# Gated linear attention, then a hard-swish MLP, on one core: the decayed keys of every chunk transposed on TensorE, under a new order of all engines

## The chip, the cores and the metric

The kernel runs on one core of a Trainium2 chip. The time is the device time of one execution in microseconds (us). Before the change the median of 7 runs is 567.04 us (565.08 to 570.57).

## The reference

The first half is a recurrence over 768 tokens for 4 batches of 8 heads with 48 dimensions; the second half is an MLP on the 3072 tokens that come out.

```python
state = zeros((B, H, D, D))                       # B 4, H 8, S 768, D 48
for t in range(S):
    state = alpha[:, :, t, :, None] * state + einsum('bhd,bhe->bhde', k[:, :, t], v[:, :, t])
    y[:, :, t] = einsum('bhd,bhde->bhe', q[:, :, t], state)
x = y.transpose(0, 2, 1, 3).reshape(3072, 384)
h = x @ w_in                                      # 384 -> 2048
g = h * clip(h + 3.0, 0.0, 6.0) / 6.0
out = g @ w_out                                   # 2048 -> 384
```

## The kernel before

**Tiling.** The tokens are cut into 24 chunks of 128 (six for each batch, numbered j from 0). Two chunks make a group g of 256 tokens, so there are 12 groups. A chunk goes through the recurrence in its parallel form: a scan over alpha gives the decay R, keys are multiplied by R and queries by its counterpart P, scores are masked, and a state of 48x48 per head is handed to the next chunk of the batch. A group then goes through the MLP. Groups 0 and 1 use plain matrix products while the weights (float64 in DRAM, taken as pairs of 32-bit words) are still being loaded and converted; from group 2 on both products run as Strassen-like schemes with fewer multiplications, so that DVE makes sums of the weights, of x and of the products.

**Steps.** Everything is written as short steps, and one long string of words, read from left to right, fixes the order of the instructions on every engine. No scheduler moves anything afterwards: an engine executes its own instructions in the order of the words and waits in place where data or a buffer isn't there. The words that matter here are:

- `la.j`, `lk.j`, `lq.j`, `lv.j.z`: loads of a chunk's alpha, keys, queries and values, all on SP's DMA queue (L256 for the first six chunks, L267 for the others, L276 and L277 for the values); `w.i`: a sixteenth of the weights, on the same queue (L174, L177), converted by `d1`, `d2`, `dx` on ACT, `d3` on DVE and `d4` on POOL.
- `ta`, `tk`, `tq`: for chunks 0 to 5 a transpose on TensorE into PSUM (L288); from chunk 6 on a DVE transpose in 32x32 blocks, since the load already put the blocks in place (L292).
- `r.j`, `p.j`: the scans on DVE (L315, L326); `k.j`, `q.j`: the products with the decays on DVE (L338); `sc.j`: scores on TensorE (L346); `m.j`: masks on DVE (L352); `yi.j`, `yx.j`: the chunk's output on TensorE (L440, L450); `cy.j`: its copy out of PSUM on ACT (L458, L459).
- `u.j`: the update of the state on TensorE (L410), which needs the decayed keys with tokens on the partitions, that is a 128x128 transpose of each of the four head pairs; `sm.j` adds it to the state on DVE (L423, L425), `st.j` decays it on POOL (L397). The last chunk of each batch (5, 11, 17, 23) has no update.
- `M`, `n`, `o`, `e`, `h`: the first product of a group and its gate (TensorE L592, ACT L598, DVE L529 to L533, ACT L487, DVE L491); `P`, `K`, `G`, `s`, `O`: the second product (TensorE L692, ACT L671, DVE L708 and ACT L705, DVE L639 and L656, store L713). `f`, `fa`, `fb`, `fr`, `fg`, `b`: the products of groups 0 and 1 (TensorE L471, L482, L509). `z.m.n`: n products of the identity with itself on TensorE (L524), whose result nobody reads; they stand in the first 40 us.

**The transposed keys before the change.** For chunks 0 to 4 the words `kb.j` and `ck.j` make them: four TensorE transposes into a PSUM bank of the pool `t` (four banks, shared with `ta`, `tk`, `tq`, the two banks of scores, `u` and the two banks of `y`) and an ACT copy of 128x512 to SBUF.

```python
def k_by_token(j):                                  # kb
    if not last(j):
        t = bank("kb", j)
        for p in range(NP):
            nc.tensor.transpose(t[:, p], K_t[j][:, p], ident)
def keep_k(j):                                      # ck
    if not last(j):
        kb_t[j] = wk.tile([C, NP, C], FP, tag="kb", name="kb")
        nc.scalar.copy(out=kb_t[j], in_=ps_t.pop(("kb", j)))
```

For chunks 6 and up that have an update (15 of them) the words `kt.j`, `kw.j` and `kr.j` take their place: a DVE transpose in 32x32 blocks into the chunk's own load buffer (L380), four DMAs of 64 KB to a DRAM tile called `far` (L387) and one DMA of 256 KB back (L391). All five DMAs are issued on SP's queue, in line with the loads.

## Time and profile before

| | before |
|---|---|
| median of 7 runs | 567.04 us |
| the profiled execution, its own time | 565.55 us |
| the profiled execution, its span | 563.7 us |
| ACT busy | 196.7 us (35%) |
| POOL busy | 55.8 us (10%) |
| DMA queue of SP and its share of the 16 engines | 48.19 MB, 40.2% |
| granted TensorE clock over the span | 0.999 |

The span runs from the first to the last instruction of the profiled execution; 1.85 us of its time lie outside of it. PE is TensorE's matrix products, PEld its loads of weights, which overlap them; DVE, ACT and POOL are the vector, scalar and general engines; SP only issues DMAs here. The end of a matmul is modelled and one overlaps the next, so the distance from one start to the next says more of its price than its duration. A wait is named by who waited, for whom, the microseconds in total, the number of times and the longest.

### The profile page before, as it was taken

The numbers are of one execution on the slowest core, as the hardware profiler recorded it, in microseconds if no ns is written. First come the engines' busy times: TensorE is split into PE (matmuls) and PEld (weight loads), VectorE is DVE, ScalarE is ACT, GpSimd is POOL, SyncE is SP. The second block draws the span as 40 slices with busy tenths as digits, with TensorE's granted clock in tenths as the row PEclk, the third lists the DMA queues.
The fourth block names the chain that finished last, engine by engine and source line by source line (L and its number), as shares of the span: only waits on it lengthen the run. The fifth ranks groups of instructions, "written<-read, shape, count | busy, mean of one in ns | idle before, by whom it ended". The sixth has DMA issues, their size and how long they took to land.

```text
span 563.7 us, 12762 instructions
## 1 busy us (share of the span) xinstructions
PE 550.8 (98%) x5236; PEld 510.5 (91%) x5236; DVE 470.2 (83%) x798; ACT 196.7 (35%) x348; POOL 55.8 (10%) x70
## 2 busy tenths in 40 slices
PE   8899999999899998999999999999999999999997
PEld 7687977699799988999999999999999999999997
DVE  7886997999999998998998978976999977754580
ACT  1476665002322333322423422432421432432420
POOL 2333445100001000100000000000000000000000
PEclk9999999999999999999999999999999999999999
DMA  9999777104524636164264353162163340000000
GB/s 148 188 174 205 203 208 197 32 16 89 132 74 96 141 74 148 52 141 88 63 150 104 76 123 82 20 165 59 45 144 81 83 121 8 1 22 8 1 30 21
DMA packets 121270, 53.73 MB, mean 95 GB/s; under 512 B 80636, under 2 KB 114172, under 8 KB 121212
## 3 DMA queue, kind: packets, MB, share of 16 engines
q1 hardware_dynamic: 114588, 48.19, 40.2%
q10 hardware_dynamic: 6624, 4.72, 2.5%
q8 instruction: 41, 0.67, 0.5%
q14 instruction: 17, 0.14, 0.1%
HBM read 44.24 MB, written 8.65 MB: 94 GB/s over the span
## 4 chain that ended last, share of the span: by engine, by line
PE 86%; DMA 10%; DVE 2%; SPq 1%; issue 1%; ACT 0%; DVEq 0%; ACTq 0%
PE m_ps L692 35%; PE m_ps L592 28%; PE m_ps L471 5%; DMA rings<-in_k_dram 4%; PE m_ps L509 4%; PE y_ps L440 3%; PE sc_ps L346 3%; PE y_ps L450 2%; DMA t<-in_v_dram 2%; PE m_ps L482 2%; PE u_ps L410 2%; DMA kb<-far 1%; DMA aq<-in_alpha_dram 1%; PE tk_ps L288 1%; DMA far<-kq 1%
## 5 line engine op out<-in xcount | busy, mean ns | idle before, releaser
L692 PE MATMUL m_ps<-w,g_sb 128*128 128x192 f32 x704 | 121.2, 328 | 0.0
L692 PEld LDWEIGHTS m_ps<-w,g_sb 128*128 128x128 f32 x704 | 113.8, 190 | 2.3 <-issue 1.4
L598 ACT COPY g_sb<-m_ps 128x512 f32<-128x512 f32 x110 | 64.3, 584 | 139.0 <-PE m_ps L592 120.6
L692 PE MATMUL m_ps<-rings,g_sb 128*128 128x192 f32 x528 | 91.2, 326 | 0.0
L692 PEld LDWEIGHTS m_ps<-rings,g_sb 128*128 128x128 f32 x528 | 85.7, 190 | 0.0
L592 PE MATMUL m_ps<-xc,w 128*128 128x128 f32 x640 | 83.1, 278 | 0.2 <-ACT g_sb L598 0.2
L592 PEld LDWEIGHTS m_ps<-xc,w 128*128 128x128 f32 x640 | 77.2, 192 | 3.3 <-issue 1.6
L487 ACT ACTIVATE r<-g_sb,half 128x512 f32<-128x512 f32 x80 | 55.5, 719 | 55.3 <-DVE g_sb L529 22.5
L491 DVE SCALAR_TENSOR_TENSOR g_sb<-r,g_sb 128x512 f32<-128x512 f32 x80 | 54.4, 698 | 7.5 <-PE m_ps L692 4.3
L397 POOL TENSOR_TENSOR t<-t,R 128x384 f32<-128x384 f32 x20 | 20.9, 1045 | 382.9 <-DVE t L425 205.6
L592 PE MATMUL m_ps<-xT,raw 128*128 128x128 f32 x400 | 51.8, 276 | 0.0
L592 PEld LDWEIGHTS m_ps<-xT,raw 128*128 128x128 f32 x400 | 48.7, 192 | 0.3
L529 DVE TENSOR_TENSOR g_sb<-m_ps,g_sb 128x512 f32<-128x512 f32 x30 | 20.4, 684 | 27.9 <-ACT g_sb L598 27.2
L592 PE MATMUL m_ps<-xT,w 128*128 128x128 f32 x320 | 41.9, 278 | 0.0
L639 DVE TENSOR_TENSOR g_sb<-g_sb 128x512 f32<-128x512 f32 (+1 forms) x55 | 41.7, 793 | 0.1
L592 PEld LDWEIGHTS m_ps<-xT,w 128*128 128x128 f32 x320 | 38.2, 192 | 1.2 <-issue 0.2
L352 DVE TENSOR_TENSOR A<-sc_ps,mask 128x512 f32<-128x512 f32 x48 | 30.8, 683 | 2.5 <-PE sc_ps L346 2.1
L592 PE MATMUL m_ps<-xc,raw 128*128 128x128 f32 x240 | 32.1, 277 | 0.7 <-ACT g_sb L598 0.7
L471 PE MATMUL m_ps<-xT,w 128*128 128x256 f32 x144 | 32.8, 382 | 0.0
L315 DVE TENSOR_TENSOR_SCAN R<-t,ones 128x516 f32<-128x516 f32 x24 | 29.4, 1224 | 3.1 <-ACT t L306 2.8
L529 DVE TENSOR_TENSOR g_sb<-g_sb 128x512 f32<-128x512 f32 x40 | 27.0, 679 | 5.5 <-ACT g_sb L598 5.4
L592 PEld LDWEIGHTS m_ps<-xc,raw 128*128 128x128 f32 x240 | 29.9, 192 | 1.2 <-ACT g_sb L598 0.9
(110 smaller groups left out, 704.4 us busy)
## 6 DMA issues: line engine op xcount, KB each, us to landing
raw<-in_moe_w_out_dram SPq DMA_DIRECT2D x8, 768.0 KB
t<-in_v_dram SPq DMA_DIRECT2D x48, 96.0 KB
raw<-in_moe_w_in_dram SPq DMA_DIRECT2D x24, 192.0 KB
out_dram<-oh ACTq DMA_DIRECT2D x44, 96.0 KB
far<-kq SPq DMA_DIRECT2D x60, 64.0 KB
kb<-far SPq DMA_DIRECT2D x15, 256.0 KB
kq<-in_k_dram SPq DMA_DIRECT2D x36, 96.0 KB
aq<-in_alpha_dram SPq DMA_DIRECT2D x36, 96.0 KB
```

Source lines behind the costliest of these rows:

```text
L315: nc.vector.tensor_tensor_scan(out=reverse(R, n - 1, n), data0=reverse(ax, n, n), data1=reverse(ones, n, n), initial=0.0, op0=ALU.mult, op ...
L352: nc.vector.tensor_tensor(out=A_t[j][:, NP * o : NP * (o + 1)], in0=ps_t.pop(("sc%d" % o, j)), in1=mask.unsqueeze(1).to_broadcast([C, NP, ...
L397: nc.gpsimd.tensor_tensor(out=st[j % 2], in0=sm[j % 2], in1=R_t[j][:, :, 0:1].to_broadcast([C, NP, 2 * D]), op=ALU.mult)
L471: nc.tensor.matmul(h[:, f], w1[:, kk, o : o + C], xT_t[g][:, kk], start=(kk == 0), stop=(kk == KT - 1))
L487: nc.scalar.activation(out=to, in_=h, func=AF.Relu, bias=half, scale=1.0 / 6.0)
L491: nc.vector.scalar_tensor_tensor(out=to, in0=r, scalar=1.0, in1=h, op0=ALU.min, op1=ALU.mult)
L509: nc.tensor.matmul(o_t[c], gs[0][:, f, c * C : (c + 1) * C], w2[:, f], start=(f == 0), stop=(f == NF - 1))
L529: eng.tensor_tensor(out=out, in0=in0, in1=in1, op=ALU.add if s1 > 0 else ALU.subtract)
L592: nc.tensor.matmul(acc[g][i][:, f * C : (f + 1) * C], spots[w][:, f * C : (f + 1) * C], x_of(g, x), start=(first and f == 0), stop=last, s ...
L598: nc.scalar.copy(out=slots[z], in_=acc[g][i])
L639: nc.vector.tensor_tensor(out=out, in0=in0, in1=in1, op=ALU.subtract)
L692: nc.tensor.matmul(to[g], a, rhs[:, f], start=(first and f == 0), stop=(last and f == HF - 1), skip_group_check=True)
```

## The change

The words `kt`, `kw` and `kr`, their functions and the pool in DRAM go. The words `kb` and `ck` now also stand for the 15 chunks that used them, so all 20 chunks with an update get four TensorE transposes and an ACT copy. The whole string of words is replaced by another one; besides the words named, the words and their numbers are the same, apart from the choice of PSUM banks and SBUF slots (the last number of several words) and the `z` words, whose products go from 28 to 33. The order differs everywhere: in the loads at the start, in which sixteenth of the weights comes first, in how far ahead chunks are prepared (chunk 13's keys, queries and scores come within group 4's products instead of group 5's), in the place of each product.

```diff
-    far = ctx.enter_context(tc.tile_pool(name="far", bufs=2, space=bass.MemoryType.DRAM))
...
-    def turn_k(j):
-        to = k_in_blocks(j).rearrange("r (v p c) -> r p v c", v=V, p=NP)
-        nc.vector.transpose(out=to, in_=K_t[j].rearrange("r p (v s) -> r p v s", v=V))
...
-    def write_k(j):
...
-    def read_k(j):
...
-        "kt": turn_k, "kw": write_k, "kr": read_k, "u": update, "sm": next_state, "yi": within, "yx": across, "cy": keep_x,
+        "u": update, "sm": next_state, "yi": within, "yx": across, "cy": keep_x,
...
-        run("""la.0 z.3.5 lq.0 lk.0 lk.1 ta.0 la.1 ca.0 tq.0 r.0 lv.0.0 tk.0 lq.2 p.0 tk.1 z.0.2
-            la.2 k.0 ta.1 q.0 z.0.1 lq.1 ca.1 sc.0 r.1 la.3 tq.2 z.0.5 m.0 lv.3.1 k.1 w.1 ta.2
...
-            xc.2.7 G.1.3 kt.6 O.1.3 xc.2.8 kw.6 tq.6 xc.2.9 y.14 M.2.7.1 n.2.0.8 xc.2.2 y.22
-            M.2.1 p.6 n.2.7.9 M.2.8 lv.6.1 n.2.1.10 o.2.4.0 M.2.2 q.6 e.2.4 y.24 sc.6 n.2.2.11
-            xc.2.10 G.1.2 ca.7 kr.6 O.1.2 M.2.3 m.6 lk.7 M.2.18.2 M.2.4 r.7 n.2.18.12 M.2.17
-            n.2.4.13 lq.7 h.2.4 M.2.19 o.2.0.0 p.7 u.6 e.2.0 M.2.9 lq.8 h.2.0 M.2.5 tk.7 yi.6
...
+        run("""la.0 z.3.5 lk.1 lq.0 la.1 ta.0 la.2 ca.0 tk.1 r.0 lk.2 tq.0 lk.0 p.0 ta.1 z.0.2 ca.1
+            lv.1.0 q.0 ta.2 r.1 z.0.2 ca.2 lq.1 tk.2 z.0.2 k.1 lv.0.1 tk.0 p.1 z.0.6 lv.3.2 k.0
+            sc.0 la.3 tq.1 w.3 r.2 z.0.7 q.1 m.0 kb.0 z.0.2 ck.0 k.2 sc.1 lq.2 p.2 ta.3 la.4 m.1
...
+            kb.6 h.2.4 la.9 M.2.2 ck.6 y.22 M.2.17 tq.7 n.2.2.11 u.6 y.24 lk.9 M.2.3 r.7
...
+            s.6.5 P.6.0.3 xc.7.7 m.16 ca.19 u.15 K.6.0 M.7.2 G.6.0 sm.15 O.6.0 P.6.2 n.7.2.15
+            st.16 r.18 M.7.3 K.6.1 p.18 P.6.4 M.7.4 M.7.7.0 n.7.4.14 kb.16 n.7.7.12 M.7.5 tk.18
+            ck.16 M.7.8 n.7.5.13 k.18 lk.20 u.16 o.7.0.0 sc.17 sm.16 e.7.0 M.7.9 st.17 lv.19.2
+            m.17 M.7.18.1 lq.19 h.7.0 yi.17 o.7.1.0 n.7.18.14 r.19 e.7.1 M.7.10 lv.18.0 yx.17
...
```

## The prediction

> **What bounds the kernel now.** I read the page's first part, then the stages, the waits, and last the prices of single steps. The first table has one row for each stretch: its length, then busy time and count for each engine, then the granted clock, the DMA share and GB/s.

> ```profile
> span 563.7 us, 12762 instructions
> ...
> 0.00:60.00 60.00, 54.05 (x580) 46.53 (x581) 45.41 (x75) 30.84 (x41) 20.03 (x31) 1.00 1.10 176
> 60.00:120.00 60.00, 60.00 (x417) 46.43 (x417) 54.22 (x77) 25.53 (x38) 20.19 (x24) 1.00 0.50 146
> 120.00:240.00 120.00, 116.11 (x1166) 109.92 (x1165) 115.73 (x200) 38.17 (x72) 6.35 (x5) 1.00 0.41 95
> 240.00:540.00 300.00, 300.00 (x2951) 287.24 (x2950) 245.74 (x435) 99.41 (x191) 9.19 (x10) 1.00 0.32 75
> ```

> The columns after the length are PE, PEld, DVE, ACT, POOL. From 240 us on PE has no hole at all, while DVE is at 82% and ACT at 33%. Between 120 and 240 us PE misses 3.89 us and DVE is nearly as full (96%). In the first 60 us PE misses 5.95 us, with the DMA engines full. So PE's own work sets the end, and the only time that a new order can win is in the first 240 us. The chain of waits says the same: 86% of it is PE.

> Next is who waits for the trip that goes, and for the loads behind it.

> ```profile
> PE u_ps L410 <- DMA aq<-in_alpha_dram: 1.6, 1, 1.6
> PE m_ps L524 <- POOL ident masks.py:199: 1.5, 1, 1.5
> ...
> PE u_ps L410 <- DMA kb<-far: 0.9, 1, 0.9
> ```

> PE waited twice at `u` for a DMA. The second is the read from `far` by name (chunk 6, near 143 us). The first is chunk 8's, near 219 us. `u` doesn't read alpha; its `kb<-far` was issued at 215.79 and the alpha loads just after it, so I read the name as a mistaken landing and count this wait to the same trip. All 13 other reads landed under cover.

> **The prices.** Groups by line first (busy us, mean ns of one | idle before), then PE's timeline around two of the existing `kb` steps (start, duration), then a product block from the chain.

> ```profile
> L380 DVE STREAM_TRANSPOSE kq<-k 128x512 f32<-128x512 f32 x15 | 10.6, 704 | 0.1
> L363 PE MATMUL kb_ps<-ident,k 128*128 128x128 f32 x20 | 3.1, 278 | 0.0
> L368 ACT COPY kb<-kb_ps 128x512 f32<-128x512 f32 x5 | 2.9, 588 | 7.1 <-PE kb_ps L363 7.1
> ```

> ```profile
> 30.36 0.60 PE L363 MATMUL kb_ps<-ident,k 128*128 128x128 f32 x4
> 30.69 1.42 PEld L482 LDWEIGHTS m_ps<-xT,w 128*128 128x128 f32 x12
> 30.80 1.50 PE L482 MATMUL m_ps<-xT,w 128*128 128x128 f32 x12
> ```

> ```profile
> 86.03 0.60 PE L363 MATMUL kb_ps<-ident,k 128*128 128x128 f32 x4
> 86.56 1.08 PE L440 MATMUL y_ps<-A,t 128*32 128x128 f32 x32
> 87.57 0.56 PE L410 MATMUL u_ps<-t,kb 128*48 128x48 f32 x16
> ```

> ```profile
> 114.33 0.89 PE m_ps L592 x8
> ```

> Four transposes are four instructions, one each, and the next block starts 0.44 us (30.36 to 30.80) or 0.53 us (86.03 to 86.56) after the first of them. A product `M` is written as four matmuls and runs as eight instructions in 0.89 us, so 0.111 us each; a `z` product (56 instructions for 28) is 0.222 us.

> **Added: 15 `kb` on PE.** 15 x 0.49 us (the middle of 0.44 and 0.53) = **+7.35 us**, ends 6.6 and 8.0. By the stages above nothing hides them from 240 us on. In the old order chunks 6 to 9 are scored before about 200 us, so at most four of the 15 (2.0 us) can fall into holes of the 120 to 240 us stretch; I count none as hidden.

> The group row gives 278 ns for one transpose, start to end. [...]

> **Added: 15 `ck` on ACT.** 15 x 0.588 = 8.8 us, off the path: ACT is busy 33% where PE is full. What it delays are the copies `n` queued behind it, and through their PSUM banks the next `M`; that is in the term for new waits.

> **Removed: 15 `kt` on DVE.** 10.6 us of busy time. From 240 us on DVE isn't the limit, worth 0. Before that it is near it, and four of them are 2.8 us; but the new order also draws chunk 13's transposes, scans and products (about 7 us of DVE work: 3 x 1.1, 1.4, 1.2, 2 x 0.7) from group 5 into group 4, and more sums of weights ahead of `P.1.4`, so DVE is relieved less in the crowded part than the removal says. I take 0; ends -2.8 and 0.

> **Removed: the trip.** SP loses 60 writes and 15 reads, each about 0.6 us of issue, and the waits of the writes for DVE, behind which loads stood:

> ```profile
> SPq L387 <- DVE kq L380: 44.1, 6, 14.4
> ...
> DVE k L292 <- DMA kq<-in_k_dram: 4.8, 4, 1.8
> ```

> SP waited long, but the loads behind it cost DVE only 4.8 us in four waits and PE nothing directly. PE gets back the two waits at `u`: 1.6 + 0.9 = 2.5, **-2.5 us**; ends -2.5 and 0 (0 if another wait takes the place).

> [...]

> **Moved: the start.** Up to the end of the first weight sixteenth SP loads 11 pieces of 0.197 MB and 0.786 MB before (2.95 MB), 12 and 0.786 after (3.15 MB): 0.2 MB, 1.1 us at 176 GB/s. Up to the sixth sixteenth it is 8.66 MB against 8.85. PE's words without `z` ahead of the product of that sixteenth are about 42 us in both. I take 0. Ends: -4.5 (the 5.95 us missing in the first 60, less the 1.47 before the first matmul) and +4.5 (one sixteenth later, 0.786 MB at 176 GB/s). The five more `z` are 1.1 us that fill waiting; 0, ends 0 and +1.1. The last group's words are the same, 0.

> **New waits.** `kb` waits for a bank, `ck` for `kb`, `u` for `ck`, where before `u` had only to find the read landed. At 86.03 to 87.57 this chain was paid in 1.54 us, with only 1.01 us of `yi` between. In the new order the shortest covers are two products, 1.78 us (chunks 6, 16, 18), at 16 with an `n` ahead of `ck` (+0.58). Chunk 17's `yi` has 1.78 us of products behind its scores, while DVE has `sm.16` and `m.17` to do (0.7 + 1.37). Behind a `yi` or `u` that waits stand all later products on PE. I take **+1.5 us**, three such places at 0.5; ends 0 and 9 (0.6 us, an ACT instruction that is in the way, for each of 15 chunks).

> **Sum.** 7.35 - 2.5 + 1.5 = +6.35. Against the profiled execution's own 565.55 us this is 571.9. That execution lies 1.49 us under the median of 567.04, so the median goes to 573.4.

> **Rivals.**

> *A wait for the new chain decides.* The row for it is ACT's 7.1 us of waiting for `kb` in front of five copies; against it, PE waited only some 0.2 to 0.4 us for ACT there, and all but a few places have over 2 us of cover. With 9 instead of 1.5: 573.4 + 7.5 = 580.9. It decides from 0.4 us a chunk.

> *The waiting that goes pays for most.* The trips, the rest of the 3.89 us and half of the start's 4.5: 567.04 + 7.35 - 3.89 - 2.25 = 568.3, no measurable difference. For it: DVE at 96% there loses four `kt`. Against it: the work drawn forward.

> *The new order of the start makes it faster.* One mechanism: loads and weights come so that PE never waits in the first 60 us and half of the 28 `z` (6.2 us) give way to work. 567.04 + 7.35 - 3.89 - 4.5 - 3.1 = 562.9. It decides only if over 10.2 us (7.35 and the 2.84 of half a per cent) are won of the 14.6 that exist there at all. Against it: the `z` grow to 33, and the loads ahead of the first weights grow.

> *The change doesn't do what it says*, that is, the transposes are hidden: the 300.00 of 300 us excludes it for 11 of 15. Only four hidden: 573.4 - 2.0 = 571.4, inside the forecast.

> **How the numbers follow.** The forecast (570 to 577) 0.60; the chain of new waits (577 to 586) 0.17; most is paid back 0.14; faster 0.09. About 0.5%, 2.8 us, is what a measurement of this kernel can tell from no change, so faster means under 564.2 and slower over 569.9: 0.09, 0.14, 0.77. The predicted time is the likeliest case's, 573.4. The range 566.5 to 580 leaves out the faster case and the upper part of the new waits.

> **What would show it.** Right: 80 instructions at L363, PE's blocks of four transposes 0.44 to 0.53 us apart from the next start, PE full from 240 us on, no wait at L410 for a DMA, SP's queue smaller by the 75 DMAs, ACT 8 to 9 us busier, DVE some 10 us less. Wrong: holes in PE after 240 us at `yi`, `u` or `kb` (then the second case), or PE's first product of the MLP several us earlier than 28.9 us and a full PE between 120 and 240 us (then the faster cases).

## The result and the profile after

The changed kernel takes 569.26 us (median of 26 runs, 568.15 to 569.80), the kernel before 567.02 us (68 runs, 563.96 to 572.26). The ratio is 1.0034, with a 95% interval of 1.0019 to 1.0049: 1.1 to 2.8 us slower, the likeliest 1.9. The forecast was 573.4 us and 6.35 us slower. The direction was right and the size three times too large. Not foreseen at all: the changed kernel's runs lie within 1.7 us of each other, those of the kernel before within 8.3.

The profiled execution took 568.15 us and its span is 566.3. First the stages of the kernel after, in the columns of before (length; busy time and count of PE, PEld, DVE, ACT, POOL; granted clock, DMA share, GB/s).

```profile
0.00:60.00 60.00, 54.58 (x593) 46.46 (x594) 49.80 (x80) 32.70 (x45) 20.09 (x33) 1.00 1.14 186
60.00:120.00 60.00, 60.00 (x427) 47.59 (x426) 55.96 (x84) 23.61 (x36) 17.23 (x23) 1.00 0.56 157
120.00:240.00 120.00, 119.33 (x1238) 112.37 (x1237) 117.30 (x192) 40.45 (x78) 4.59 (x5) 1.00 0.32 78
240.00:540.00 300.00, 299.87 (x2906) 287.18 (x2905) 234.29 (x412) 103.95 (x197) 10.52 (x10) 1.00 0.20 51
```

PE missed 3.89 us between 120 and 240 us before; now it misses 0.67. From 240 us on it is as full as before (0.13 us missing), so the new steps brought no wait there. The first 60 us look much alike (5.42 against 5.95 us).

The groups of the added steps, then all of PE's own waits except those under 0.3 us:

```profile
L362 PE MATMUL kb_ps<-ident,k 128*128 128x128 f32 x80 | 12.1, 273 | 0.0
L367 ACT COPY kb<-kb_ps 128x512 f32<-128x512 f32 x20 | 11.9, 593 | 13.1 <-PE kb_ps L362 13.0
```

```profile
PE tq_ps L287 <- DMA rings<-in_q_dram: 2.2, 2, 1.7
PE m_ps L499 <- POOL ident masks.py:199: 1.5, 1, 1.5
PE tk_ps L287 <- DMA rings<-in_k_dram: 0.8, 2, 0.5
PE ta_ps L287 <- DMA rings<-in_alpha_dram: 0.5, 1, 0.5
PE m_ps L567 <- DVE g_sb L504: 0.4, 1, 0.4
```

There are 80 transposes instead of 20, none with idle time before it, and no update waits for a DMA. Counting from the start of each block to the start of the next, the transposes take 9.7 us of PE in this trace and 2.4 in that of before: +7.3. The same count over all blocks, against the price that such a block has when PE is full (near the shortest that occurs), gives the time that PE loses: 26.6 us before, 21.8 after, of which 11.8 and 9.3 lie in the first 60 us and 8.3 and 4.9 between 120 and 240 us. These are counts over all starts of the trace, not a row of it; the totals depend on the price that is taken, the difference of 4.8 little (4.3 to 5.6 us with prices from the shortest to the median). The fillers `z` are 10 instructions more, at 0.11 us each 1.1 us. Of the 7.3, 6.5 are the transposes' price when PE is full (60 at 0.109 us from start to start) and 0.8 the switches between blocks, which the count of lost time contains: 6.5 + 1.1 - 4.8 = 2.8, against the 2.6 between the two spans. So the transposes cost what was forecast, and about 5 us came back instead of the net 1.0 of the forecast.

### The profile page after: what moved, and what is told of

It is laid out like the page before. It is cut to its first block, busy times and chain, and to the rows that moved or that the text cites. A ratio compares the mean times of both kernels' runs of the same rounds, so it can differ in the third digit from the quotient of the medians.

```text
span 566.3 us, 12769 instructions
## 1 busy us (share of the span) xinstructions
PE 557.2 (98%) x5306; PEld 516.8 (91%) x5306; DVE 468.3 (83%) x783; ACT 204.7 (36%) x363; POOL 52.4 (9%) x70
## 4 chain that ended last, share of the span: by engine, by line
PE 93%; DMA 3%; DVE 2%; SPq 1%; ACT 0%; issue 0%; DVEq 0%; ACTq 0%
PE m_ps L667 35%; PE m_ps L567 31%; PE m_ps L446 6%; PE sc_ps L345 4%; PE y_ps L415 4%; PE m_ps L484 4%; PE y_ps L425 2%; PE m_ps L457 2%; PE u_ps L385 1%; DMA rings<-in_k_dram 1%; PE kb_ps L362 1%; PE m_ps L499 1%; DMA rings<-in_alpha_dram 1%; SPq L266 1%; PE tk_ps L287 0%; DMA aq<-in_alpha_dram 0%
## 5 line engine op out<-in xcount | busy, mean ns | idle before, releaser
L567 PE MATMUL m_ps<-xc,w 128*128 128x128 f32 x640 | 84.3, 279 | 0.4 <-DVE g_sb L504 0.4
L462 ACT ACTIVATE r<-g_sb,half 128x512 f32<-128x512 f32 x80 | 57.5, 723 | 72.1 <-DVE g_sb L508 37.4
L504 DVE TENSOR_TENSOR g_sb<-g_sb 128x512 f32<-128x512 f32 x40 | 28.2, 716 | 4.3 <-ACT g_sb L573 4.2
L325 DVE TENSOR_TENSOR_SCAN P<-t 128x516 f32<-128x516 f32 x24 | 30.6, 1273 | 0.1
```

Of the source, the lines that this page charges most:

```text
L325: nc.vector.tensor_tensor_scan(out=P_t[j], data0=aX[j % 2][:, 0:n], data1=ini[j % 2], initial=0.0, op0=ALU.mult, op1=ALU.add)
L462: nc.scalar.activation(out=to, in_=h, func=AF.Relu, bias=half, scale=1.0 / 6.0)
L504: eng.tensor_tensor(out=out, in0=in0, in1=in1, op=ALU.add if s1 > 0 else ALU.subtract)
L567: nc.tensor.matmul(acc[g][i][:, f * C : (f + 1) * C], spots[w][:, f * C : (f + 1) * C], x_of(g, x), start=(first and f == 0), stop=last, s ...
```

## The experiments

Theory 1, formed on that: the transposes cost PE their 7.3 us in full, and the new order takes waits away. Theory 2: the end of the trip paid, by its load, whatever the order. Theory 3: a part of the transposes is hidden. Ratios are to the kernel before on the same chip, with their 95% interval; "us" behind a ratio is worked out with 567.

**The transposes alone, in the old order.**

```diff
-    kt.6 ... kw.6 ... kr.6 ... u.6        (and so for all 15 chunks)
+    ... kb.6 ck.6 ... u.6                 (kb, ck where kr stood)
```

> The old order, with the trip's words taken out and kb, ck in the place where the read stood. Theory 1 (the 15 transposes cost their 7.3 us on PE in full, and the new order takes waits away, 2.5 us of them at the start): the trip's own two waits go, so 567.0 + 7.3 - 2.5 = 571.8, PE still misses about 5.9 us of the first 60 us, and PE's blocks at the kb line add up to about 9.7 us. Theory 2 (it was the end of the trip, with its load on DMA, SP and DVE, that paid, not the order): 569.3, as the changed kernel. Theory 3 (a part of the transposes is hidden, so they cost PE less than 7.3 us): under 569.

Measured: 569.93 us, 1.0062 (1.0040 to 1.0083), +3.5 us (2.3 to 4.7). Its stages:

```profile
120.00:240.00 120.00, 119.09 (x1196) 113.19 (x1195) 114.36 (x195) 40.89 (x78) 6.34 (x5) 1.00 0.33 80
240.00:540.00 300.00, 299.73 (x2954) 286.41 (x2954) 239.19 (x420) 101.56 (x197) 9.17 (x10) 1.00 0.20 51
```

PE has its 119.09 us between 120 and 240 us without any new order; by starts it loses 4.6 us there (8.3 before). The price of 7.35 less the measured 3.5 makes the trip worth 3.9 us, not 2.5. That is most of what came back, and theory 2 has the larger part. (At the same granted clock it is 3.1 us, see the end of this section.) And the chain `kb`, `ck`, `u`, set into an order that wasn't made for it, brings no wait after 240 us.

**The new order with the trip back for 11 chunks.**

```diff
-    ... kb.7 ... ck.7 ... u.7             (chunks 7, 9, 10, 12 to 16, 18, 21, 22)
+    k.7 kt.7 ... kw.7 ... kr.7 ... u.7    (kt into a tile of its own)
```

> The new order, with the trip through DRAM back for the 11 chunks whose keys are ready over 60 words ahead of the update (7, 9, 10, 12 to 16, 18, 21, 22), in a buffer of its own; chunks 6, 8, 19, 20 keep the transposes. Theory 1: PE loses 11 x 0.486 = 5.3 us and nothing waits for the reads: 569.3 - 5.3 = 563.9, faster than both kernels. Theory 2: the trip's load comes back, with 11 of 15 of its price: 567 or more. Theory 3: between 564.5 and 567, since PE gets back less than 5.3 us.

Measured: 572.84 us, 1.0111 (1.0080 to 1.0141), slower than both. PE got back its transposes (4.8 us by starts against 9.7) and lost 10.2 us more elsewhere, here after 240 us too:

```profile
240.00:540.00 300.00, 295.45 (x2850) 281.32 (x2849) 237.70 (x417) 97.69 (x186) 11.12 (x10) 1.00 0.27 65
```

```profile
PE m_ps L687 <- DVE g_sb L526: 1.2, 2, 0.8
PE m_ps L587 <- DVE xc L526: 1.1, 1, 1.1
```

PE waits for DVE there, in a stretch where DVE has 62 us to spare. The trip was put into the order by hand, and its DVE transposes and DMAs delay DVE's work of other chunks (DVE waits 3.1 us for loads between 240 and 540 us, in the changed kernel for none); which of the two does it wasn't separated. Theory 1's "nothing waits" is wrong for this run; it shows how little the order tolerates, not the price of a trip that was planned for.

**Only the new start, and only the new rest.** The words up to `M.2.15` (or `P.1.1`) from one kernel, the rest from the other, each word once, with PSUM bank numbers matched at the seam. In the first of the two, chunk 8 is computed from wrong keys: the new start loads them before `kt.6` of the old rest writes into the same buffer. The steps are the same, so its time still counts here.

```diff
-    la.0 z.3.5 lq.0 lk.0 lk.1 ta.0 ... b.1.3 y.3 | y.7 y.4 ...  (old | old)
+    la.0 z.3.5 lk.1 lq.0 la.1 ta.0 ... y.6 y.2   | y.7 y.4 ...  (new | old, with the trip)
+    la.0 z.3.5 lq.0 lk.0 lk.1 ta.0 ... y.11 y.15 y.13 | xc.2.0 ...  (old | new, with kb)
```

> The new order up to the last words before the first Strassen product (M.2.15), then the old order with the trip. Theory 1: the start's part alone, 2.5 us of waits less and 1.1 us of fillers more, -1.4: 565.6. Theory 2: 567.0, since the trip is still there. Theory 3 says nothing of it.

> The old order up to the first word of the second product (P.1.1), then the new order with the transposes. Theory 1: the changed kernel without the start's gain, 569.3 + 1.4 = 570.7. Theory 2: 569.3, as the changed kernel.

Measured: new start, old rest 566.18 us, 0.9991 (0.9965 to 1.0018); old start, new rest 572.66 us, 1.0099 (1.0065 to 1.0132). The first is no measurable gain beside the trip. The second, +5.6 us (3.7 to 7.5), lies at or above the +3.5 of the old order with transposes: behind the start, the new order is worth nothing that could be seen, and the gain that theory 1 gave to it falls. But it also lies 3.7 us above the changed kernel (1.0099 against 1.0034), from which only the start differs. So the start is worth nothing ahead of the old rest and more ahead of the new one, or the seam has a price of its own; that wasn't separated.

**Is the price the two waits, or the load?** First the two updates that waited, later on PE. (The second is chunk 10's: it stands right ahead of `sc.10` in the trace. The prediction called it chunk 8's.)

```diff
-    ... u.6 e.2.0 M.2.9 ... M.2.5 ...     ... u.10 k.11 n.4.4.8 sc.10 ... M.4.5 ... M.4.9 ...
+    ... e.2.0 M.2.9 ... M.2.5 u.6 ...     ... k.11 n.4.4.8 sc.10 ... M.4.5 ... M.4.9 u.10 ...
```

> The old order with the trip; only the updates u.6 and u.10, the two that waited for the read, stand later on PE, behind two more products (u.6) or the scores and two products (u.10). Theory 1a (what the trip cost PE was those two waits, 3.0 us by PE's starts: 1.2 and 1.8 over the blocks' own time): about 3 us faster than the kernel before, 563.4 to 564. Theory 2a (the trip costs by its load on DVE, SP and DMA, and the waits are only where that shows): within 1 us of the kernel before, and other waits between 120 and 240 us.

Measured: 568.20 us, 0.9993 (0.9961 to 1.0024), no gain. Its stretch from 120 to 240 us, and PE's waits over the whole execution:

```profile
120.00:240.00 120.00, 116.85 (x1166) 109.93 (x1165) 115.83 (x198) 37.18 (x72) 6.34 (x5) 1.00 0.42 95
```

```profile
PE m_ps L592 <- ACT g_sb L598: 2.3, 4, 0.7
```

No update waits for the read any more, and PE still misses 3.15 us: the products now wait for PSUM copies on ACT (2.3 us in four waits), which wait for DVE at some of them (7.4 us in two waits between 120 and 240 us). By starts PE loses 8.2 us there, as before (8.3). The waits at `u` were where the lateness showed, not its cause.

Then the trip's parts, added to the old order with transposes, their results unread:

```diff
+    kt.6 ... kb.6 ck.6 ... u.6                       (and_kt: DVE's part)
+    kt.6 ... kw.6 ... kr.6 kb.6 ck.6 ... u.6         (and_trip: all of it)
```

> The old order with the transposes on PE (as old_order_kb), and beside them the 15 DVE transposes of the trip, whose result nobody reads. Theory 1a: as old_order_kb, +0 to +0.3 us. Theory 2a, by DVE: the 0.7 us between the 3.0 of the two waits and the 3.7 that PE won between 120 and 240 us come back, +0.7 or more.

> The old order with the transposes on PE, and beside them the whole trip (DVE transpose, four writes, the read into a buffer that nobody reads). Theory 1a: as old_order_kb within 1 us, since nobody waits for the read. Theory 2a: +2 to +4 us over old_order_kb, the trip's price without a wait of PE for it.

Measured, on one chip: with `kt` 571.28 us, 1.0043 (1.0016 to 1.0070); with the whole trip 572.59 us, 1.0069 (1.0044 to 1.0095). The intervals overlap each other and that of the run without either. The stretch from 120 to 240 us is clearer, first with `kt`, then with the trip:

```profile
120.00:240.00 120.00, 118.59 (x1191) 112.48 (x1190) 116.44 (x200) 40.48 (x78) 6.34 (x5) 1.00 0.33 77
```

```profile
120.00:240.00 120.00, 117.08 (x1177) 110.57 (x1176) 114.81 (x196) 39.52 (x75) 6.35 (x5) 1.00 0.43 95
```

PE's busy time falls from 119.09 to 118.59 to 117.08, and to the 116.11 of before, where the update also reads from the trip. By starts PE loses 4.6, 5.3, 7.4 and 8.3 us: 0.7 for DVE's transposes, 2.1 for the DMAs that nobody waits for, 0.9 for the reads themselves; each step is one profile against another. At the same granted clock (end of this section) the times say so too: 569.3 us without the trip, 569.5 with `kt`, 572.1 with the whole trip. The trip was paid mainly by its load, in the one stretch where DVE and PE are both nearly full (115.73 and 116.11 of 120 us before).

**The trip's DMAs on another queue.**

```diff
-            nc.sync.dma_start(out=to[o], in_=src[BLK * o : BLK * (o + 1)])
+            nc.gpsimd.dma_start(out=to[o], in_=src[BLK * o : BLK * (o + 1)])
...
-        nc.sync.dma_start(out=kb_t[j]...
+        nc.gpsimd.dma_start(out=kb_t[j]...
```

> The kernel before, with the trip's five DMAs a chunk issued on POOL's queue instead of SP's, so that no load of keys, queries, values or alpha stands behind a write that waits for DVE. If the trip's price without a wait for its read (2.1 us from old_order_kb_and_kt to old_order_kb_and_trip, in PE's holes between 120 and 240 us) is loads held up in SP's line: these loads come in time, PE misses 2 us less there, and the time is 1 to 2 us under the kernel before. If it is the transfers' own load on the DMA engines: as the kernel before within 0.5 us. If POOL is too slow as an issuer (its st.j stand behind the issues): slower than before, with POOL's waits in front of yx.

Measured: 568.02 us, 1.0019 (0.9995 to 1.0044). The halves of the stretch go opposite ways (120 to 180, 180 to 240 us):

```profile
120.00:180.00 60.00, 55.66 (x494) 53.16 (x493) 54.63 (x98) 15.37 (x31) 8.08 (x15) 0.97 0.38 79
180.00:240.00 60.00, 59.65 (x660) 55.98 (x659) 59.31 (x97) 20.96 (x38) 14.76 (x19) 1.00 0.53 120
```

In the second half PE is busy 59.65 us (58.08 before) although more bytes move in it (120 GB/s, 105 before), as if the loads had been held up behind the writes in SP's line. In the first half the read for chunk 6 comes still later (issued at 140.50 us, 136.83 before) and PE waits 3.3 us at `u`. The total decides nothing; that loads wait in SP's line is likely, not shown.

**The price of a transpose, doubled.**

```diff
-            for p in range(NP):
-                nc.tensor.transpose(t[:, p], K_t[j][:, p], ident)
+            for _ in range(1 if j < FIRST else 2):
+                for p in range(NP):
+                    nc.tensor.transpose(t[:, p], K_t[j][:, p], ident)
```

> The changed kernel with the four transposes of the 15 later chunks done twice into the same bank. Theory 1: 60 more transposes at 0.11 us back to back, +6.5 us (the block's own switch is paid once), 575.8. Theory 3 (a part of the transposes falls into holes of PE): +5 us or less.

Measured: 574.85 us (574.56 to 575.76), 1.0118 (1.0086 to 1.0151). That is 5.6 us over the changed kernel's median for 60 transposes, 0.093 us each; by the two ratios it is 4.8, which hang on the kernel before and its wide spread. By starts the blocks grew by 6.1 us; the 0.67 us that PE missed between 120 and 240 us are gone:

```profile
120.00:240.00 120.00, 120.00 (x1249) 113.27 (x1248) 116.28 (x190) 40.56 (x79) 4.58 (x5) 1.00 0.33 78
```

So they are paid nearly in full, and only a hole that is there takes a little of them. Theory 3 is out as the reason of the small loss: the starts show +7.3 for the 60 of the change and +6.1 for these.

**No fillers.**

```diff
-    la.0 z.3.5 lk.1 lq.0 la.1 ta.0 la.2 ca.0 tk.1 r.0 lk.2 tq.0 lk.0 p.0 ta.1 z.0.2 ca.1
+    la.0 lk.1 lq.0 la.1 ta.0 la.2 ca.0 tk.1 r.0 lk.2 tq.0 lk.0 p.0 ta.1 ca.1
```

> The changed kernel without its 33 filler products z (56 us later than here nobody reads them). If the fillers hold the granted clock at the start: the clock falls under 1.00 somewhere in the first 60 us, and the time goes up by 1 us or more, with a wider spread than the 1.7 us of the changed kernel's 26 runs. If they only fill waiting: within 0.5 us of the changed kernel. If they stood in the way of work: up to 1 us faster.

(The bracket in it is a slip; it means products whose result nobody reads.)

Measured: 569.36 us (568.65 to 569.90), the changed kernel's time and its narrow spread. The row of the first 60 us has 1.00 for the clock, but this profile holds no record of the clock before 25.15 us, and the starts say otherwise. Here are two blocks of four transposes, each with the block behind it (start, duration), one before and one after that time:

```profile
17.41 1.12 PE L362 MATMUL kb_ps<-ident,k 128*128 128x128 f32 x4 [0.78 <-DVE q L337]
18.45 2.81 PE L345 MATMUL sc_ps<-q,k 48*128 48x128 f32 x16
```

```profile
39.59 0.60 PE L362 MATMUL kb_ps<-ident,k 128*128 128x128 f32 x4
40.12 0.56 PE L385 MATMUL u_ps<-t,kb 128*48 128x48 f32 x16
```

The same block takes 1.04 us and then 0.53. So at 17.41 us PE ran at half the speed of 39.59 us, and the record of a full clock begins at 25.15; in the changed kernel the transposes start 0.213 us apart until 4.7 us and 0.109 from 5.8 us on. With the fillers the full speed thus comes 12 to 19 us earlier (an estimate from 17.41, 25.15 and near 6 us), and that is worth nothing in the time here (569.26 us with them, 569.36 without). Afterwards they aren't what keeps it: all 12 runs have a mean clock of 1.000 on record.

**A version that beats both.** Transposes where the trip's load hurts, the trip where PE is full; then the new start ahead of it.

```diff
-    kt.6 ... kw.6 ... kr.6 ... u.6        (chunks 6 to 10)
+    ... kb.6 ck.6 ... u.6
     kt.12 ... kw.12 ... kr.12 ... u.12    (chunks 12 to 22 keep the trip)
```

> The old order; transposes on PE for the five chunks 6 to 10, whose trips run in the stretch of 120 to 240 us where DVE is nearly full, the trip for the ten chunks from 12 on, which run where PE is full. If the trip's load is what cost PE its 3.7 us there, and costs nothing later: 5 x 0.49 - 3.7, so 1.2 us faster than the kernel before. If the trip costs evenly in every chunk (3.7 / 15 each): 2.4 - 1.2, so 1.2 us slower.

> The same, behind the new order of the start (up to M.2.15; chunk 8's keys are loaded where the old order has them). The start's part: no fall of the granted clock between 20 and 50 us in any run, so a narrow spread, and 0.5 to 1.5 us on the median: some 2 us faster than the kernel before. If the start is worth nothing: as old_order_kb_6_to_10.

Measured: in the old order 565.29 us, 0.9936 (0.9906 to 0.9965); behind the new start 564.49 us, 0.9923 (0.9893 to 0.9952), with 12 runs between 563.14 and 565.48. Its stretches:

```profile
120.00:240.00 120.00, 119.09 (x1195) 113.17 (x1194) 113.64 (x186) 40.72 (x77) 6.42 (x5) 1.00 0.28 66
240.00:540.00 300.00, 300.00 (x2951) 287.25 (x2950) 245.68 (x435) 99.36 (x191) 9.17 (x10) 1.00 0.33 75
```

PE has the 119 us of the transposes in the crowded stretch, and after 240 us the trip runs without a hole. The first run's 3.6 us (2.0 to 5.3) are more than the 1.2 that were expected: the runs of the kernel before beside these two have a higher median than elsewhere (567.96). With both at a full clock the gain is 2.1 us, and 2.0 behind the new start, so the new start adds nothing there.

**The same runs at a full clock.** Every run has its mean granted clock on record, and a fall to half for 3.41 us (last section) takes 0.003 off it. Of the 97 runs of the kernel before beside these experiments, 24 have 0.999 or more and a median of 565.3 us; 33 have 0.996 or 0.997 and 567.4; 40 have less and 569.4. So its wide spread is mostly the clock, and its median holds some 2 us of it. Of the changed kernel's 27 runs with a clock on record, 17 have 1.000 (568.9 us) and 10 have 0.996 or 0.997 (569.6). Medians of the runs with 0.999 or more alone, each beside the kernel before on its chip:

| | its runs | kernel before | difference |
|---|---|---|---|
| transposes in the old order | 569.3 (5) | 565.0 (8) | +4.3 |
| old start, new rest | 571.7 (4) | 565.0 (8) | +6.6 |
| with `kt`, unread | 569.5 (5) | 565.1 (3) | +4.3 |
| with the whole trip, unread | 572.1 (6) | 565.1 (3) | +7.0 |
| transposes for chunks 6 to 10 | 563.9 (5) | 566.0 (8) | -2.1 |
| the same behind the new start | 564.1 (7) | 566.0 (8) | -2.0 |
| no fillers | 569.4 (12) | 566.0 (8) | +3.3 |
| new start, old rest | 565.7 (4) | 565.0 (8) | +0.6 |
| updates later | 566.9 (4) | 565.1 (3) | +1.8 |
| doubled transposes | 574.7 (4) | 565.1 (3) | +9.6 |
| trip back for 11 chunks | 572.7 (5) | 565.0 (8) | +7.7 |
| the change itself | 568.9 (17) | 565.3 (24, all chips) | +3.6 |

The groups are small, and the kernel before differs by 1 us between chips. The unread trip costs 2.7 us beyond `kt`, without a wait of PE for it. And the change costs 3.6 us rather than 1.9 where the clock doesn't fall.

## Why the prediction was wrong in size

- **The transposes, +7.35.** Right: +7.3 by PE's starts, and doubled they cost nearly their price again. The page's duration of one (278 ns, 16.7 us for 60) was rightly not taken as the price: the blocks of four have the next block's start 0.44 to 0.53 us behind their own. The clock of 1.00 in the row of the first 60 us doesn't hold for all 92 of the old kernel's transposes (72 at L288, 20 at L363): its profile has no record of the clock before 10.2 us, and until then transposes start 0.213 us apart (0.109 later). The price came from blocks at 30 and 86 us and isn't touched by it.
- **The copies on ACT, off the path.** Right: ACT 8.0 us busier, PE full from 240 us on.
- **The trip, -2.5.** Mis-sized: some -3.9 (7.35 less the 3.5 measured with the transposes alone; the interval leaves -2.7 to -5.1), or -3.1 at a full clock. The step read the price off two waits at `u` and counted 13 trips as free because nobody waited for them. That is the step that failed, more than its size: taking those waits away won nothing, and the load of the trips in the crowded stretch was the price. Ends of -2.5 and 0 for this term were too tight.
- **`kt` on DVE, 0.** Mis-sized a little: 0.7 us by PE's starts, which the -3.9 contains (0.2 by the times at a full clock).
- **New waits, +1.5.** This step failed too: they are none. PE misses 0.13 us after 240 us, and even the untuned places for `kb` and `ck` brought nothing. The covers that I found short (1.78 us) sufficed.
- **The start, 0.** About -1.6 us (1.9 for the change less 3.5 for the transposes in the old order), a difference of two intervals that don't exclude 0. At a full clock it is -0.4 (568.9 against 569.3). Beside the trip the new start showed nothing (0.9991), beside the five transposes nothing at a full clock; only ahead of the new rest it looks like more (2.7 to 3.7 us, with the seam in it). Of the 2.5 us that PE lost less in the first 60 us, some 1.9 (an estimate: 18 instructions fewer at half speed, 0.213 instead of 0.109 us for each) come from the full speed near 6 instead of 10.2 us, and in the run without fillers a full speed that came 12 us later or more cost no time (569.36 us).
- **The clock, not in the sum.** The step from the profiled execution to the median (+1.49) carried the median of the kernel before over to the changed kernel, and with it falls of the clock that the changed kernel has more seldom (10 of its 27 runs have a mean clock under 0.999, 73 of 97 of the kernel before). The change costs 3.6 us at a full clock and 1.9 over all runs; the 1.7 between them are this, as far as groups of this size tell.
- **The rest of the new order.** Rightly given nothing of its own.

The sum with these is 7.35 - 3.9 + 0 - 1.6 = +1.9; -3.9 and -1.6 are differences of measured times, so that it comes out is no test. At a full clock it is 7.35 - 3.1 - 0.4 = +3.9, beside the 3.6 above. The case that I named "the waiting that goes pays for most" (568.3 us, a chance of 0.14) had the better mechanism, and its row, DVE at 96% between 120 and 240 us, was the one to trust. That the time came so near it is partly luck: it counts 1.2 us, and 1.7 of what came back is the clock, which it doesn't have. The size of the forecast rested on the two terms that failed and on a median with the clock in it.

## What to carry to other kernels

Here a transfer for which nobody waited still had a price (2.1 us by PE's starts) where the engines beside it were nearly full; it was read from the holes of that stretch, and moving the wait away didn't win it back (0.9993). Price the same step stage by stage: work on the full engine was worth paying where its alternative crowded two others, and not where that alternative was hidden, so that a mixture beat both (0.9936, behind the new start 0.9923). Where a new wait is only feared, its bound belongs into the range rather than into the sum. And before two medians are compared, sort the runs by their granted clock: between the changed kernel and the one before, how often it fell differed (10 of 27 runs, 73 of 97).

## What the runs showed of the hardware

The granted clock isn't the same in all runs of one start. In five of the eight profiles with the old start it fell for some microseconds, most often between 20 and 50 us; in none of the six with the new start. Over all runs on record it is rarer there rather than gone: 49 of 75 runs with the new start have a mean clock of 0.999 or more, and 54 of 174 with the old one. Here are a fall (the old order with transposes and `kt`) and a stretch with nearly as little work on PE in which the clock stayed (the same with the whole trip):

```profile
24.02:27.43 3.41, 1.60 (x40) 0.86 (x34) 1.89 (x2) 0.26 (x2) 2.57 (x1) 1.00 1.22 192
27.43:34.26 6.83, 6.83 (x51) 6.51 (x52) 4.25 (x7) 2.50 (x5) 1.15 (x2) 0.50 0.86 168
```

```profile
22.51:25.93 3.42, 1.64 (x36) 1.23 (x36) 1.95 (x3) 1.74 (x1) 1.60 (x1) 1.00 1.07 194
25.93:29.34 3.41, 2.78 (x59) 2.12 (x60) 1.40 (x3) 0.54 (x2) 0.22 (x1) 1.00 1.06 128
```

The spread itself is the second surprise. Kernels whose updates read all 15 trips spread over 8.3 us (before, 68 runs), 8.1 (updates later, 12), 6.5 (trip on POOL's queue, 12) and 5.9 (new start, 12); the changed kernel over 1.7 (26), without fillers over 1.3 (12), with doubled transposes over 1.2 (6). Most of it is the clock, by the table above. Why the kernels that read the trip have more falls isn't shown.
